# Efficient attention with mixture of depths: q of units 5 to 15 loaded as two shifted copies and transposed by VectorE

## The chip, the cores and the metric

The kernel runs on one core of one Trainium2 chip. The metric is the device time of one execution in microseconds (us). The kernel before took 209.97 us (median of 3 runs, 209.13 to 210.23).

## The reference

Two steps. The first is an attention that takes no scores between queries and keys: q is softmaxed over its 64 features, k over the 576 tokens, k and v are multiplied into a 64 x 64 matrix for each head, and q is multiplied with that matrix. The second is a mixture of depths: a gate scores the 576 tokens of a batch, and only the 128 best go through a two-layer MLP, whose result is added to their rows.

```python
q, k, v: (8 batches, 8 heads, 576 tokens, 64), float32
q_s = softmax(q, axis=features);  k_s = softmax(k, axis=tokens)
kv  = einsum('bhsd,bhse->bhde', k_s, v)
x   = einsum('bhsd,bhde->bhse', q_s, kv)     # then (8, 576, 512): heads side by side
scores = x @ w_gate
top = 128 best tokens of each batch
out = x;  out[top] = x[top] + sigmoid(scores[top]) * (relu(x[top] @ w1) @ w2)   # w1 512x1024, w2 1024x512
```

## The kernel before

**Units.** The attention is cut into 16 units of four heads: unit u is half of the heads of one batch, so two units make a batch. Everything is float32, except for small masks. A head's 576 tokens are 64 partitions of T = 9 consecutive tokens each.

**Loads.** `load` (L115) brings k, v and q of a unit into three rotating sets of buffers, `raw` (L105; unit u uses set u % 3). All are issued from SP's queue in program order. From unit 2 on, k and v are loaded with 64 partitions of the tile (every second one) in each of two DMAs, in rows of 1280 and 1024 bytes (L141); q with all 128 partitions, in two DMAs of 5 and 4 tokens a partition (L135). Units 0 and 1 (`FLAT`) are loaded in another form (L129).

**A unit's work.** `k_exp` and `q_exp` take the exps on ScalarE (L268, L276), `v_copy` moves v beside a column of ones (L281). `kv_mm` (L310) multiplies exp(k) with v on TensorE, `kv_out` (L319 to L323) divides by the sums on VectorE and appends the product with the gate. `q_t` turns exp(q) so that features lie on the partitions: for the units from 3 on, 18 transposes of 64x128 on TensorE into PSUM (L349), and two copies from PSUM into `qT` (part 0 by ScalarE, L356; part 1 by ScalarE or, from unit 5 on, by VectorE, L354). `x_mm` (L375) multiplies with the 64x66 result of `kv_out`: 36 products for each unit, of which each has 64 tokens as its weights. `x_sums` and `x_scale` (L389 to L395) divide by the sums, and `x_store` (L405) writes the unit's rows to the output in HBM: two DMAs, each from 64 neighbouring partitions.

**Selection.** After the second unit of a batch, `score` and `score_row` (L414 to L438) lay the scores out, `ranks` compares every score with all others (five compares of 128x576 on VectorE, L446), `hits` and `find` (L463, L473) give the indices of the 128 best, `fetch` (L487) gathers their rows from the output by an indirect DMA on POOL, which has to wait for the batch's two stores.

**MLP.** `turn` (L524) transposes the gathered rows, `mlp1` (L544) and `mlp2` (L554) are the two layers in eight pieces each, `finish` (L567) adds, and `put` (L559) scatters the rows back.

**Order.** The order on every engine is the program's, written out by hand. From s = 3 on (`LAG`) a loop runs one stage for each unit. Stage s transposes unit s (`q_t`), does `kv_mm` of unit s + 1, `x_mm` of unit s, its sums and scaling, then `queues` (L762): the store of unit s, and the loads of k, v and q of unit s + 3, the first of which waits for the last of `x_mm`. Then come the exps of q of unit s + 1 and of k of unit s + 2, and the copy of v of unit s + 2. Pieces of the MLP of an earlier batch lie in between: odd stages hold layer 1 and the ranks, even stages layer 2 and the next `turn`. The units before that stage are written out one by one (L683 to L741), as is stage 3 (L785 to L829).

The core of the loop's stage, where the change falls:

```python
            if here:
                q_t(s, 0)
                q_t(s, 1, on_vector=s > LAG + 1)
            if follows:
                kv_mm(s + 1)
                kv_out(s + 1)
```

The functions that the diff touches, with the line numbers of the profile:

Of the kernel before, what the change touches and what calls it, by code (L numbers as in the profile page):

```python
# [8 lines left out]
F32 = mybir.dt.float32  # L9
BF16 = mybir.dt.bfloat16  # L10
I32 = mybir.dt.int32
AF = mybir.ActivationFunctionType
# [5 lines left out]
def kernel(  # L18
# [23 lines left out]
    nc = tc.nc  # L42
    B, H, S, D = q.shape
    DM, F = moe_w1.shape
    P = 128
    R = 5
    N2 = R - 1
    T = R + N2
    RP = N2 * P + P // 2
# [3 lines left out]
    SD = S * D  # L53
# [18 lines left out]
    const = ctx.enter_context(tc.tile_pool(name="const", bufs=1))  # L72
    ld = ctx.enter_context(tc.tile_pool(name="ld", bufs=3))
    at = ctx.enter_context(tc.tile_pool(name="at", bufs=2))
    xp = ctx.enter_context(tc.tile_pool(name="xp", bufs=2))
    md = ctx.enter_context(tc.tile_pool(name="md", bufs=2))
# [3 lines left out]
    def bank(tag, bufs):  # L80
        return ps.tile([P, 512], F32, tag=tag, name=tag, bufs=bufs)

    def pair(tag, bufs=1):
        return ps.tile([P, 2, 512], F32, tag=tag, name=tag, bufs=bufs)
# [4 lines left out]
    def part(i):  # L89
        return slice(64 * i, 64 * i + 64)  # L90
# [7 lines left out]
    NU = len(units)  # L98
# [2 lines left out]

    LD = 3
    FLAT = 0, 1
    RR = 4 * R
    raw = {w: [const.tile([P, 2 * T if w == "q" else RR, D], F32, name=f"{w}{n}") for n in range(LD)] for w in "qkv"}  # L105

    def view(t, paired):
        return t.rearrange("p (h r) d -> p h r d", h=4) if paired else t[:, :2 * T].rearrange("p (i r) d -> p i r d", i=2)
# [6 lines left out]
    def load(u, which, after=None, split=False, flat=False):  # L115
        b, qd = units[u]
        for what in which:
            src = {"q": q, "k": k, "v": v}[what]
            first = src[place(b), 4 * qd].offset
            dmas = []  # L120
            if flat:
                t = view(raw[what][u % LD], False)
                if split:
                    for h, queue in enumerate((nc.scalar, nc.sync)):
                        dmas.append(queue.dma_start(out=t[:, h].rearrange("p r d -> p (r d)"),
                                                    in_=bass.AP(tensor=src.tensor, offset=first + 2 * h * SD,
                                                                ap=[[T * D, P], [1, T * D]])))
                else:
                    dmas.append(nc.sync.dma_start(out=t.rearrange("p i r d -> p i (r d)"),  # L129
                                                  in_=bass.AP(tensor=src.tensor, offset=first,  # L130
                                                              ap=[[T * D, P], [2 * SD, 2], [1, T * D]])))
            elif what == "q":
                t = view(raw[what][u % LD], False)
                for r0, r1 in ROWS:
                    dmas.append(nc.sync.dma_start(out=t[:, :, r0:r1].rearrange("p i r d -> p i (r d)"),  # L135
                                                  in_=bass.AP(tensor=src.tensor, offset=first + r0 * D,
                                                              ap=[[T * D, P], [2 * SD, 2], [1, (r1 - r0) * D]])))
            else:
                t = view(raw[what][u % LD], True)
                for n, rows in ((1, N2), (0, R)):  # L140
                    dmas.append(nc.sync.dma_start(out=t[n::2, :, :rows].rearrange("p h r d -> p h (r d)"),  # L141
                                                  in_=bass.AP(tensor=src.tensor, offset=first + n * R * D,
                                                              ap=[[T * D, 64], [SD, 4], [1, rows * D]])))
            if after is not None:
                behind(dmas[0], after)
                after = None
        return dmas[-1]

    ROWS = (0, R), (R, T)
    ctx.enter_context(tc.manual_schedule())  # L150
    load(0, "k", split=True, flat=True)
    load(0, "vq", flat=True)

    def clear(u):
        for what in "kv":
# [5 lines left out]
                                               ap=[[DM, 1], [1, DM]]))  # L161
# [18 lines left out]
    ones_b = const.tile([P, 4 * P], BF16, name="ones_b")  # L180
    nc.vector.memset(ones_b, 1.0)
    w_ps = bank("mm", 2)
    ones_f = const.tile([P, 4 * P], F32, name="ones_f")
    nc.gpsimd.memset(ones_f, 1.0)
    for n in range(WARM):
        nc.tensor.matmul(out=w_ps, lhsT=ones_f[:, :P], rhs=ones_f, start=True, stop=True)
# [20 lines left out]
    for n in range(2):  # L207
        t = const.tile([P, RR, D + 1], F32, name=f"v_ones{n}")
        nc.vector.memset(t[:, :, D:], 1.0)
        v_ones.append(t)  # L210
        t = const.tile([P, 2, C], F32, name=f"kv_w{n}")
        nc.vector.memset(t[:, :, D:D + 1], 1.0)
        kv_w.append(t)
    qrec = const.tile([P, NU, 2, G], F32, name="qrec")
    krec = const.tile([P, NU, 2], F32, name="krec")


    order_minus_p = const.tile([P, RP], F32, name="order_minus_p")
    nc.gpsimd.iota(order_minus_p, pattern=[[1, RP]], base=0, channel_multiplier=-1,
                   allow_small_or_imprecise_dtypes=True)  # L220

# [39 lines left out]
    st = {}  # L261
# [9 lines left out]
    def q_exp(u, c):  # L271
        if c == 0:
            st["qe", u] = at.tile([P, T, 2, D], F32, tag="qe", name="qe")
        r0, r1 = ROWS[c]
        qr = raw["q"][u % LD].rearrange("p (i r) d -> p r i d", i=2)
        nc.scalar.activation(out=st["qe", u][:, r0:r1], in_=qr[:, r0:r1], func=AF.Exp)  # L276

    def v_copy(u, engine=nc.scalar):
# [44 lines left out]
        nc.vector.reduce_sum(out=kw[:, :, D + 1], in_=prod, axis=AX.X)  # L323


    copies = []

    def q_t(u, c, on_vector=False, wide=False, later=False):
# [29 lines left out]
    def x_mm(u, a, wide=False, tag="x"):  # L358

        qT = st["qT", u] if a == 0 else st.pop(("qT", u))  # L360
        x = pair(tag, 2 if tag == "x" else 1)
        kw = kv_w[u % 2]
        for r in range(R):
            for i, c in QUARTERS:
                to = x[part(c), i, r * C:(r + 1) * C]
                if r == N2 and c:
                    last = nc.tensor.matmul(out=to, lhsT=ones_b[part(i), :D], rhs=ones_b[part(i), :C], start=True, stop=True)
                    continue
                if wide and r < N2:
                    if c == 0:  # L370
                        nc.tensor.matmul(out=x[:, i, r * C:(r + 1) * C],
                                         lhsT=qT[part(i), a, r].rearrange("p c t -> p (c t)"), rhs=kw[part(i), a],
                                         start=True, stop=True)
                    continue
                nc.tensor.matmul(out=to, lhsT=qT[part(i), a, r, c], rhs=kw[part(i), a], start=True, stop=True)  # L375
        st["x", u, a] = x[:, :, :R * C].rearrange("p i (r c) -> p i r c", r=R)
        return last

# [113 lines left out]
    def select(b, n, r):  # L492

        k0, m = slots[n]
        if r == 0:
            st["select", n] = bank("mm", 2), md.tile([P, R, P], F32, tag="hit_f", name="hit_f", bufs=1)
        t_ps, hit = st["select", n]
        far = md.tile([P, P], F32, tag="far", name="far")
        nc.scalar.activation(out=far[:, :m], in_=slot_no[:, k0:k0 + m], func=AF.Abs, scale=-1.0,
                             bias=st["rank", b][:, r:r + 1])  # L500
        nc.scalar.activation(out=hit[:, r, :m], in_=far[:, :m], func=AF.Relu, scale=-1.0, bias=1.0)
        row = xs[b][:, r].rearrange("p n i a d -> p (n i a d)")
        for d in range(KD):
            nc.tensor.matmul(out=t_ps[:, d * m:(d + 1) * m], lhsT=row[:, d * P:(d + 1) * P], rhs=hit[:, r, :m],
                             start=(r == 0 and d == 0), stop=(r == N2 and d == KD - 1), skip_group_check=True)
        if r == N2:
            turned(b, n, t_ps)
# [74 lines left out]
    def each(step, b, *args):  # L582
        for n in range(n_sl):
            step(b, n, *args)
# [93 lines left out]
    for h in range(2):  # L678
        nc.tensor.matmul(out=g_ps[part(h), :4 * D], lhsT=ones_f[:1, :D],
                         rhs=w_row.rearrange("o (n i x) -> o i n x", i=2, x=2 * D)[:, h], start=True, stop=True)  # L680
# [61 lines left out]
    LAG = 3  # L742
# [3 lines left out]
    for s in range(LAG, NU + LAG):  # L746
# [5 lines left out]
        def pieces(n, to=None):  # L752
            nonlocal f_next
            for _ in range(n if to is None else max(0, to - f_next)):
                each(piece, mlp_b, f_next)
                f_next += 1

        here, follows = s < NU, s + 1 < NU
        ends = s // 2 if here and s % 2 == 1 else None
# [18 lines left out]
        def rows():  # L778
            score_row(ends)

        def ranks(n0=0, n1=R):
            for r in range(n0, n1):
                compare(ends, r)
# [46 lines left out]
        else:  # L830
            if chosen is not None and s not in AFTER:
                pieces(1 if here else 2)
                search()
            if here:
                q_t(s, 0)
                q_t(s, 1, on_vector=s > LAG + 1)
            if follows:
                kv_mm(s + 1)
                kv_out(s + 1)
# [21 lines left out]
            pieces(0, to=2 if follows else 3)  # L861
            if ends is not None:
                rows()
                ranks()
            if s + 2 < NU:
                k_exp(s + 2)
            pieces(0, to=4)
# [4 lines left out]
                number = count_good(good)  # L872
            if ends is not None:
                each(hits, ends)
            pieces(0, to=KF - 1)
            if second and mlp_b + 1 < B:
                each(turn, mlp_b + 1)
# [35 lines left out]
```

## Time and profile before

| | |
|---|---|
| Median of 3 runs | 209.97 us |
| The profiled execution | 210.15 us, its span 208.4 us |
| Busy: TensorE (PE) | 193.6 us, 93% |
| Busy: VectorE (DVE) | 119.0 us, 57% |
| Busy: ScalarE (ACT) | 92.1 us, 44% |
| Busy: GpSimd (POOL) | 32.4 us, 16% |
| DMA | 46.66 MB, 224 GB/s over the span |
| Time to landing of a q load | 6.2 us (median) |

The profile is that of one execution. The span runs from its first to its last instruction, and the execution's time holds 1.75 us more. Busy times of different engines overlap, so they do not add up to the span. "PE" are the matmuls, "PEld" the loads of their weights. A group of instructions is written as line, engine, operation, what it writes and reads, shape and count; then its busy time in us, the mean in ns of one, and the idle time of the engine ahead of it with what ended most of it. A window gives the busy time of PE, PEld, VectorE, ScalarE and GpSimd, then the share of TensorE's clock, the mean busy share of the 16 DMA engines, and GB/s. In the row of 40 slices one digit is a tenth of busy share.

### The profile page before, as it was taken

Reading aid. Unit: us, or ns where it says so; the run is one execution under the profiler, and the core shown is the slowest. Engines: PE = TensorE matmul, PEld = TensorE weight load, DVE = VectorE, ACT = ScalarE, POOL = GpSimd, SP = SyncE. Lnnn points to the kernel's source line nnn. Section 1 sums busy time; section 2 is a strip of 40 time slices with the busy share of each in tenths; the row PEclk is TensorE's granted clock in tenths of the full one; section 3 lists DMA queues with packets and bytes.
Section 4 is the critical chain, followed back from the end, with each engine's and each line's share of the span. In section 5 each row is a group of like instructions: output and inputs, shape, how many; then the busy total and the mean of one; then the engine's idle time right before and its main releaser. Section 6 shows DMA issues by size and latency. Waiting matters only on the chain.

```text
span 208.4 us, 6943 instructions
## 1 busy us (share of the span) xinstructions
PE 193.6 (93%) x2955; PEld 148.8 (71%) x2955; DVE 119.0 (57%) x361; ACT 92.1 (44%) x135; POOL 32.4 (16%) x93
## 2 busy tenths in 40 slices
PE   7899799798989999999999999999999999999960
PEld 3486789785579848985698759974898579659520
DVE  6668735597167645776378717862776537714010
ACT  3468876574526624545434813672464022111100
POOL 5103000202010101210120104010211012126010
PEclk9999999999999999999999999999999999999995
DMA  6999999999786999995989779895880433131101
GB/s 218 397 307 330 384 360 372 371 381 329 193 296 158 309 327 250 283 279 170 233 282 253 231 175 304 212 314 129 256 247 4 103 110 74 48 101 53 58 5 53
DMA packets 37720, 46.66 MB, mean 224 GB/s; under 512 B 2353, under 2 KB 33073, under 8 KB 37682
## 3 DMA queue, kind: packets, MB, share of 16 engines
q1 hardware_dynamic: 36256, 41.66, 65.2%
q0 software_dynamic: 1280, 4.20, 5.7%
q8 instruction: 25, 0.41, 0.8%
q10 hardware_dynamic: 146, 0.30, 0.5%
q14 instruction: 13, 0.11, 0.2%
HBM read 34.61 MB, written 11.53 MB: 221 GB/s over the span
## 4 chain that ended last, share of the span: by engine, by line
PE 74%; DMA 16%; SPq 3%; issue 1%; ACT 1%; DVE 1%; POOL 0%; POOLq 0%; ACTq 0%
PE mm L544 25%; PE mm L554 25%; DMA k<-in_k_dram 15%; PE x L375 8%; PE kv L310 8%; PE x L349 4%; DMA xr<-out_dram,idx 2%; SPq L141 2%; PE kv L432 2%; PE mm L524 2%; SPq L135 1%; ACT ke L268 1%; PE mm L473 1%; SPq L169 0%; SPq L129 0%
## 5 line engine op out<-in xcount | busy, mean ns | idle before, releaser
L544 PE MATMUL mm<-xT,w 128*128 128x128 f32 x512 | 62.0, 278 | 0.3 <-DVE xT L532 0.3
L544 PEld LDWEIGHTS mm<-xT,w 128*128 128x128 f32 x512 | 58.8, 192 | 2.0 <-ACT xT L532 0.6
L554 PE MATMUL mm<-w,hT 128*128 128x512 f32 x128 | 59.3, 599 | 0.0
L446 DVE SCALAR_TENSOR_TENSOR junk<-srow,s,not_before 128x576 bf16<-128x576 f32 x40 | 32.7, 819 | 9.4 <-ACT srow L438 8.1
L554 PEld LDWEIGHTS mm<-w,hT 128*128 128x128 f32 x128 | 22.6, 190 | 20.6 <-issue 20.1
L567 DVE SCALAR_TENSOR_TENSOR o<-mm,g,xr 128x512 f32<-128x512 f32 x7 | 5.3, 751 | 35.6 <-PE mm L554 35.6
L395 DVE TENSOR_TENSOR xs<-x,qrec 128x640 f32<-128x640 f32 x31 | 24.1, 815 | 0.0
L375 PE MATMUL x<-kv_w,qT 64*64 64x66 f32 x1084 | 21.9, 222 | 1.7 <-issue 1.5
L268 ACT ACTIVATE ke<-k 128x1280 f32<-128x1280 f32 (+1 forms) x16 | 20.0, 1253 | 4.6 <-DMA k<-in_k_dram 4.6
L276 ACT ACTIVATE qe<-q 128x640 f32<-128x640 f32 (+1 forms) x32 | 20.1, 676 | 3.3 <-DMA q<-in_q_dram 3.3
L375 PEld LDWEIGHTS x<-kv_w,qT 64*64 64x64 f32 x1084 | 19.4, 134 | 3.0 <-issue 2.0
L310 PE MATMUL kv<-v_ones,ke 128*64 128x65 f32 x560 | 19.4, 224 | 1.1 <-ACT srow L438 1.1
L310 PEld LDWEIGHTS kv<-v_ones,ke 128*64 128x64 f32 x560 | 17.5, 137 | 2.3 <-ACT srow L438 1.3
L547 ACT ACTIVATE hT<-mm 128x512 f32<-128x512 f32 x16 | 9.6, 597 | 21.5 <-PE mm L544 21.5
L281 ACT COPY v_ones<-v 128x1280 f32<-128x1280 f32 x14 | 17.6, 1257 | 0.7 <-DMA v<-in_v_dram 0.4
L532 ACT COPY xT<-mm 128x512 f32<-128x512 f32 x7 | 4.1, 585 | 30.1 <-PE mm L524 30.1
L487 POOL DMA_INDIRECT xr<-out_dram,idx x8 | 8.3, 1036 | 53.4 <-PE x L349 22.6
L559 POOL DMA_INDIRECT out_dram<-o,idx x7 | 7.0, 996 | 58.9 <-DVE o L567 58.9
L356 ACT COPY qT<-x 128x640 f32<-128x640 f32 (+1 forms) x17 | 11.4, 682 | 9.5 <-PE x L349 8.7
L438 ACT ACTIVATE srow<-kv 128x576 f32<-128x576 f32 x7 | 4.5, 648 | 23.0 <-PE kv L432 23.0
L349 PEld LDWEIGHTS x<-ident,qe 64*128 64x128 f32 x234 | 8.3, 138 | 4.9 <-ACT xT L532 4.5
L354 DVE COPY qT<-x 128x512 f32<-128x512 f32 x11 | 7.6, 692 | 5.8 <-PE x L349 5.8
(115 smaller groups left out, 165.7 us busy)
## 6 DMA issues: line engine op xcount, KB each, us to landing
out_dram<-xs SPq DMA_DIRECT2D x16, 320.0 KB, 3.6
k<-in_k_dram SPq DMA_DIRECT2D x14, 320.0 KB, 5.1
v<-in_v_dram SPq DMA_DIRECT2D x14, 320.0 KB, 6.1
q<-in_q_dram SPq DMA_DIRECT2D x14, 320.0 KB, 6.2
w<-in_moe_w_dram SPq DMA_DIRECT2D x8, 512.0 KB, 7.6
out_dram<-xs SPq DMA_DIRECT2D x16, 256.0 KB, 4.3
k<-in_k_dram SPq DMA_DIRECT2D x14, 256.0 KB, 4.8
v<-in_v_dram SPq DMA_DIRECT2D x14, 256.0 KB, 4.7
```

Of the source, the lines that this page charges most:

```text
L268: nc.scalar.activation(out=ke, in_=view(raw["k"][u % LD], u not in FLAT), func=AF.Exp)
L276: nc.scalar.activation(out=st["qe", u][:, r0:r1], in_=qr[:, r0:r1], func=AF.Exp)
L281: engine.copy(out=out_v, in_=in_v)
L310: nc.tensor.matmul(out=kv_ps[part(i), a, :D + 1], lhsT=ke[:, 2 * i + a, r], rhs=vo[:, 2 * i + a, r], start=(r == 0), stop=(r == N2))
L349: nc.tensor.transpose(out=src[:, a, r], in_=qe[part(a), r0 + r].rearrange("p i d -> p (i d)"), identity=ident[part(a), part(a)])
L356: nc.scalar.copy(out=to, in_=src)
L375: nc.tensor.matmul(out=to, lhsT=qT[part(i), a, r, c], rhs=kw[part(i), a], start=True, stop=True)
L395: nc.vector.tensor_mul(xs[b][:, :, qd, :, a].rearrange("p r i d -> p i r d"), st.pop(("x", u, a))[:, :, :, :D], rec.to_broadcast([P, 2, R, ...
L446: nc.vector.scalar_tensor_tensor(junk, st["srow", b], st["s", b][:, r:r + 1], not_before[:, r], op0=OP.subtract, op1=OP.is_ge, accum_out=s ...
L544: st["piece"] = nc.tensor.matmul(out=h_ps[:, f % 4 * m:(f % 4 + 1) * m], lhsT=w1[:, d, f * P:(f + 1) * P], rhs=xT[:, d, :m], start=(d == 0 ...
L547: nc.scalar.activation(out=hT[:, f - 3:f + 1, :m], in_=h_ps[:, :4 * m].rearrange("p (f c) -> p f c", f=4), func=AF.Relu)
L554: st["piece"] = nc.tensor.matmul(out=st["y", b, n][:m], lhsT=st["hT", b, n][:, f, :m], rhs=w2[:, f], start=(f == 0), stop=(f == KF - 1))
```

## The change

For units 5 to 15 (`TWICE`), q is loaded twice, into a buffer of double size. A head's 576 tokens are now 32 partitions of 18 consecutive tokens; the next 32 partitions hold the same tokens, starting 32 elements (half of a token's 64 features) later. So the first 32 columns of each token hold features 0 to 31 on the first 32 partitions, and features 32 to 63 on the next 32. Four DMAs bring a unit, each with 64 partitions of 1120 elements (4480 bytes). `q_exp` takes the exp of only these first halves, again 2 x 576 elements a partition. The new `q_blocks` transposes them on VectorE in 32x32 blocks, one instruction for each half of the unit, straight into `qT`, which leaves each token's 64 features on 64 partitions. `q_t` is no longer called for these units. `q_blocks(s + 1, ...)` is called in stage s: the first half after the q exps, ahead of the ranks where there are any; the second half straight after it, or after `hits` in stages that have ranks. The half of q's buffers that is now added also serves earlier as the place of `ones_f`, `order_minus_p`, `hit_f` and `far`, which had tiles of their own.

```diff
+    TWICE = range(5, NU)
     RR = 4 * R
-    raw = {w: [const.tile([P, 2 * T if w == "q" else RR, D], F32, name=f"{w}{n}") for n in range(LD)] for w in "qkv"}
+    raw = {w: [const.tile([P, 4 * T if w == "q" else RR, D], F32, name=f"{w}{n}") for n in range(LD)] for w in "qkv"}
+
+    spare = {n: raw["q"][n].rearrange("p r d -> p (r d)")[:, 2 * T * D:] for n in range(LD)}
...
+            elif what == "q" and u in TWICE:
+                t = raw[what][u % LD].rearrange("p (a n) d -> p a (n d)", a=2)
+                for a in range(2):
+                    for i in range(2):
+                        dmas.append(nc.sync.dma_start(out=t[part(i), a, :ROW],
+                                                      in_=bass.AP(tensor=src.tensor, offset=first + (2 * i + a) * SD,
+                                                                  ap=[[D // 2, 2], [2 * T * D, 32], [1, ROW]])))
             elif what == "q":
...
+    ROW = 2 * T * D - D // 2
...
-    ones_f = const.tile([P, 4 * P], F32, name="ones_f")
+    ones_f = spare[2][:, :4 * P]
...
+    for n in range(LD):
+        nc.gpsimd.memset(spare[n][:, ROW:], 0.0)
...
-    order_minus_p = const.tile([P, RP], F32, name="order_minus_p")
+    order_minus_p = spare[2][:, 4 * P:4 * P + RP]
...
     def q_exp(u, c):
         if c == 0:
             st["qe", u] = at.tile([P, T, 2, D], F32, tag="qe", name="qe")
+        if u in TWICE and u not in FLAT:
+            half = raw["q"][u % LD].rearrange("p (a n) (h s) -> p a n h s", a=2, h=2)[:, c, :, 0]
+            to = st["qe", u].rearrange("p r i d -> p (r i d)").rearrange("p (a n s) -> p a n s", a=2, n=2 * T)
+            nc.scalar.activation(out=to[:, c], in_=half, func=AF.Exp)
+            return
...
+    def q_blocks(u, a):
+        if u not in TWICE:
+            return
+        if a == 0:
+            st["qT", u] = at.tile([P, 2, R, 2, D], F32, tag="qT", name="qT")
+        to = st["qT", u].rearrange("p a r c d -> p a (r c d)")[:, :, :T * D].rearrange("p a (j t e) -> p a e j t", j=T, e=2)
+        qe = st["qe", u].rearrange("p r i d -> p (r i d)").rearrange("p (a e j s) -> p a e j s", a=2, e=2, j=T)
+        nc.vector.transpose(out=to[:, a], in_=qe[:, a])
...
     def x_mm(u, a, wide=False, tag="x"):
...
+        by_token = qT.rearrange("p a r c d -> p a (r c) d")
...
-                nc.tensor.matmul(out=to, lhsT=qT[part(i), a, r, c], rhs=kw[part(i), a], start=True, stop=True)
+                rows = by_token[part(i), a, R * c + r] if u in TWICE and u not in FLAT else qT[part(i), a, r, c]
+                nc.tensor.matmul(out=to, lhsT=rows, rhs=kw[part(i), a], start=True, stop=True)
...
-            st["select", n] = bank("mm", 2), md.tile([P, R, P], F32, tag="hit_f", name="hit_f", bufs=1)
+            st["select", n] = bank("mm", 2), spare[1][:, :R * P].rearrange("p (r t) -> p r t", r=R)
...
-        far = md.tile([P, P], F32, tag="far", name="far")
+        far = spare[1][:, (R + r % 2) * P:(R + r % 2 + 1) * P]
...
-            if here:
+            if here and s not in TWICE:
                 q_t(s, 0)
-                q_t(s, 1, on_vector=s > LAG + 1)
+                q_t(s, 1)
...
             if ends is not None:
                 rows()
+            if follows:
+                q_blocks(s + 1, 0)
+            if ends is not None:
                 ranks()
+            else:
+                q_blocks(s + 1, 1)
...
             if ends is not None:
                 each(hits, ends)
+                q_blocks(s + 1, 1)
```

More of the change, by code (lines that the diff above doesn't have):

```diff
@@ L273, in q_exp @@
             st["qe", u] = at.tile([P, T, 2, D], F32, tag="qe", name="qe")
+        if u in TWICE and u not in FLAT:
[3 more added lines that the diff above has]
+            return
         r0, r1 = ROWS[c]
-        qr = raw["q"][u % LD].rearrange("p (i r) d -> p r i d", i=2)
+        qr = raw["q"][u % LD][:, :2 * T].rearrange("p (i r) d -> p r i d", i=2)
         nc.scalar.activation(out=st["qe", u][:, r0:r1], in_=qr[:, r0:r1], func=AF.Exp)
```

## The prediction

> **What bounds the kernel now.** I read the chain of work that ended last first, since it says whose time is the run's time. Then the costliest groups, for the price of what is removed, and the slices and windows, for the DMA engines.
>
> ```profile
> PE 74%; DMA 16%; SPq 3%; issue 1%; ACT 1%; DVE 1%; POOL 0%; POOLq 0%; ACTq 0%
> ...
> L375 PE MATMUL x<-kv_w,qT 64*64 64x66 f32 x1084 | 21.9, 222 | 1.7 <-issue 1.5
> ...
> L349 PEld LDWEIGHTS x<-ident,qe 64*128 64x128 f32 x234 | 8.3, 138 | 4.9 <-ACT xT L532 4.5
> L354 DVE COPY qT<-x 128x512 f32<-128x512 f32 x11 | 7.6, 692 | 5.8 <-PE x L349 5.8
> ```
>
> The loads carry the chain for the first 40 us (DMA 16%, the q, k and v of the first units); after that TensorE is the bound. The transposes to be removed are L349's: 18 for each unit, 13 units. The chain in order of time shows what one unit's transposes are worth on that path:
>
> ```profile
> 113.09 0.86 PE mm L554 x2
> 114.13 0.71 PE x L349 x18
> 114.84 1.32 PE kv L310 x40
> ```
>
> 0.71 us, and 0.18 us idle ahead of them (113.95 to 114.13). So a unit has about 0.89 us of L349 on the path. VectorE and ScalarE are busy 57% and 44% and have room. The DMA engines are the third resource, and the fullest:
>
> ```profile
> DMA  6999999999786999995989779895880433131101
> ```
>
> Nine tenths or more in most slices up to about 150 us. The windows say what that share carries:
>
> ```profile
> 30.00:40.00 10.00, 9.86 (x257) 9.39 (x254) 6.06 (x22) 5.91 (x10) 0.92 (x5) 1.00 1.07 369
> 107.00:117.50 10.50, 10.50 (x197) 9.55 (x195) 7.64 (x21) 6.95 (x10) 1.62 (x4) 1.00 0.90 258
> 117.50:129.50 12.00, 12.00 (x170) 8.12 (x171) 6.75 (x20) 3.88 (x6) 1.93 (x6) 1.00 0.75 220
> 131.20:134.20 3.00, 3.00 (x30) 3.00 (x29) 2.89 (x8) 2.37 (x3) 0.00 (x0) 1.00 0.92 192
> ```
>
> The last two columns are the mean busy share of the 16 engines and GB/s. Two units in steady state (107 to 129.5 us) use 0.90 x 10.5 + 0.75 x 12 = 18.5 us of all 16 engines, so 9.2 us for a unit that TensorE finishes in 11.2. The last line is a stretch that holds only stores of xs, each from 64 neighbouring partitions: engines 92% busy, yet 192 GB/s, against 369 GB/s where loads over all 128 partitions run.
>
> [...] The trace's best slice, 397 GB/s, is 24.8 GB/s for each of 16; I use 24.8.
> [...]
>
> **The change, part by part.**
>
> *TensorE.* 11 units x 18 = 198 of L349's 234 matmuls go: 11 x 0.89 = 9.8 us off TensorE's path. x_mm keeps its count and its 64x64 weights.
>
> *ScalarE and VectorE.* Eleven copies of 692 ns leave each (L356, L354). VectorE gains 22 transposes of 128x576 f32. The nearest row is L395 (128x640 f32, 815 ns), so 815 x 576/640 = 0.73 us each; [...]. VectorE has 14.0 us busy in the 22.2 us of two units (129.5 to 151.7): it loses 2 x 0.69, gains 4 transposes, and becomes the bound only from (22.2 - 12.6)/4 = 2.4 us each. Half a unit's transpose also delays the ranks: q_blocks(s + 1, 0) comes ahead of them, where VectorE idles 1.07 us for srow before the first compare (130.79 us), which covers it. The exps keep their 1152 elements a partition. I put all this at 0; TensorE covers it.
>
> *Start.* Three memsets of 32 columns on POOL, and ones_f, order_minus_p, hit_f and far in the unused half of q's buffers. Their readers are done by about 30 us; the first doubled load into q2 is issued at 39 us, that into q1 at 57 us. 0.
>
> *SP.* Two q issues for a unit become four, 22 more of about 0.5 us; SP idles several us in each unit. 0 as issues, but see next.
>
> *The q loads.* Each of the four DMAs has source dimensions 2, 32, 1120 and a destination of 64 partitions by 1120. The slowest source dimension is 2. [...] each runs on two engines, and on the same two every time. A unit's q is then 4 x 64 x 4480 B = 1.147 MB, 573 KB for each of the two: at 24.8 GB/s 23.1 us [...]. The same two engines also carry their sixteenth of k, v, the stores and the gathers. q is a quarter of the bytes behind the 9.2 us, so the rest is 7 us. **A unit costs those engines about 30 us where TensorE takes 11.** [...]
>
> Nothing covers that. These DMAs, k and v and the stores are behind one another in SP's queue; queues(s) issues x(s), k, v(s + 3), q(s + 3) after x_mm(s), so two units of loads always stand ahead. q_exp(u) waits for its q, and ScalarE is then held in front of k_exp, v_copy and the MLP's evacuations, VectorE in front of ranks; TensorE idles some 20 us for each unit.
>
> Sum. The first such load follows the stores at 38.83 us:
>
> ```profile
> 38.83 1.73 SPq L135 DMA_DIRECT2D q<-in_q_dram  x2
> 40.65 1.63 SPq L405 DMA_DIRECT2D out_dram<-xs  x2
> 42.56 1.89 SPq L141 DMA_DIRECT2D k<-in_k_dram  x2
> ```
>
> Unit 5's q lands at 41 + 23 = 64 us, unit 15's at 64 + 10 x 30 = 364. Behind it in the queue is unit 13's store (2 to 3 us to land), which batch 6's gather needs (1.0 us on POOL, 4.8 to land), so that turn comes 9 us later. Before, the turn of batch 6 starts at 167.2 us and the span ends at 208.4: 41.2, less 0.9 for unit 15's transposes, 40.3. 364 + 9 + 40 = 413 us of span. The profiled execution lasted 210.15 us, 1.75 more than its span, and the median of the runs is 209.97: 415 us.
>
> One term is open on both sides. [...] by the 192 GB/s at 0.92 busy, 13.0 GB/s each, so 44 us for a unit's q instead of 23. If that held for all eleven units, 415 + 11 x 21 = 646. [...] I charge half a unit's contention, 10 us: **425 us**.
>
> **Rivals.**
> - *All sixteen engines serve the load* (the split follows the 64 partitions of the destination). For: no trace of before shows k = 2, and loads and stores with 64 outermost run wide. Against: the source's outer 2. Then q takes 1.147 MB/369 GB/s = 3.1 us of the engines in place of 2.2, so 10.1 a unit, just under TensorE's 11.2 - 0.9 = 10.3. Time 210 - 9.8 = 200, with some waits for late k 202: **faster**. With k engines the unit needs 1147/(24.8k) + 7 us; that stays under 11.2 from k = 11, so sixteen decides for faster and eight (12.8) already for slower.
> - *VectorE becomes the bound*: [...] At 3.0 us each, VectorE needs 12.6 + 12 = 24.6 us for two units instead of 22.2, so 5.5 x 2.4 = 13 us: 223. Nothing in the profile speaks for it; it also needs sixteen engines.
> - [...]
>
> **How the numbers follow.** Two engines: 0.90, most of it between 415 and 500, with a thin part up to 646. Sixteen engines and faster: 0.07. Sixteen with nothing gained, or VectorE or DMA as a mild bound: 0.03, of which 0.01 within 0.5% (about what a measurement of this kernel can tell from no change). [...] The upper end, 630, takes in contention in nearly every unit. Left out: 0.10 of other cases, and about 0.1 of the two-engine one at its edges.
>
> **What would show it.** Right: q's time to landing 20 us or more instead of 6.2; the chain mostly DMA q<-in_q_dram from 60 us on; the mean DMA share falling to a third while the run lengthens; ACT qe waiting for q about 15 us for each unit; qe's starts 28 to 50 us apart; DVE transposes near 0.73 us. Wrong: q landing in 5 to 9 us means that the loads are spread, and the time is then near 202[...].

## The result, and the profile after

The kernel after takes **401.5 us** (median of 4 runs, 400.41 to 401.65); the kernel before took 209.64 us beside it (median of 4). The ratio is 1.914 (95% interval 1.907 to 1.921). The profiled execution after has a span of 399.9 us. The forecast was 425 us, with a range of 366 to 630.

The lines have moved: q's load is now L139, its exp L290, VectorE's transpose L351, `x_mm` L404, the gather L516, the store L434, `turn` L553, the two MLP layers L573 and L583.

First the shares of the chain of waits that ended last, by engine and then by line:

```profile
DMA 70%; PE 16%; SPq 7%; ACT 3%; DVE 2%; issue 1%; POOL 0%; POOLq 0%; ACTq 0%; DVEq 0%
DMA q<-in_q_dram 60%; DMA out_dram<-xs 8%; PE mm L573 5%; SPq L434 4%; PE mm L583 3%; SPq L139 3%; DMA xr<-out_dram,idx 2%; PE mm L533 1%; PE x L404 1%; ACT qe L290 1%; PE mm L197 1%; PE x L369 1%; PE kv L328 1%; ACT srow L467 1%; PE kv L323 1%
```

Before, this line began with PE 74% and DMA 16%. Now q's loads alone are 60% of the run. The same chain in order of time (start, length, what):

```profile
97.12 26.81 DMA q<-in_q_dram
...
124.01 0.69 ACT qe L290
...
184.15 27.85 DMA q<-in_q_dram
...
327.20 24.77 DMA q<-in_q_dram
...
352.05 0.69 ACT qe L290
...
354.23 3.44 DMA xr<-out_dram,idx
...
357.81 1.09 PE mm L553 x4
```

Each load of q stands on the chain for 25 to 28 us, and the exp (`ACT qe`) follows when it lands. The second exp of unit 5 starts at 67.39 us, that of unit 15 at 352.05: 28.5 us for a unit. After that comes the end that the prediction described: unit 15's exp, a gather, the `turn` of batch 6 at 357.81, and the rest of the MLP.

The slices, and two windows of this steady part (the first number after the span's length is PE's busy time; the last three are the granted clock, the mean busy share of the DMA engines, GB/s):

```profile
PEclk9989995597775695865695955875955967759997
DMA  8999444244244356243352352451443432413110
```

```profile
156.20:241.40 85.20, 37.06 (x461) 25.59 (x461) 23.77 (x65) 15.07 (x20) 3.35 (x9) 0.70 0.38 112
241.40:352.00 110.60, 50.51 (x652) 37.57 (x652) 30.92 (x84) 19.30 (x25) 6.70 (x18) 0.72 0.37 110
```

From 40 us on (the fifth digit of the slices) the DMA share falls from 9 to about 4 tenths, and 112 GB/s flow where 369 did, while q's loads are what everything waits for. A third of the engines' time busy and yet a DMA bound: that fits a few busy engines, and the packet records (below) count them. The wait list says who stands still (total us, times, longest):

```profile
ACT qe L290 <- DMA q<-in_q_dram: 198.6, 22, 12.4
POOL xr L516 <- DMA q<-in_q_dram: 194.0, 5, 44.1
PE mm L553 <- DMA xr<-out_dram,idx: 117.9, 7, 20.8
```

ScalarE waits 198.6 us for q in 22 waits. The two waits below it are what follows from that: the stores that a gather needs are issued from the same queue, behind loads of q (the releaser named is q's DMA), and TensorE's `turn` waits 117.9 us for gathered rows. The groups of the exp and of the new transposes:

```profile
L290 ACT ACTIVATE qe<-q 128x576 f32<-128x576 f32 x22 | 15.0, 683 | 198.6 <-DMA q<-in_q_dram 198.6
...
L351 DVE STREAM_TRANSPOSE qT<-qe 128x576 f32<-128x576 f32 x22 | 17.1, 776 | 87.3 <-ACT qe L290 87.3
```

The exps cost what they did (683 ns; 676 before). The transposes cost 776 ns each, 17.1 us in all, and their idle time is that of the exps: VectorE is not what is late.

### The profile page after: what moved, and what is told of

Same layout as the page of the kernel before. It is cut to its first block, busy times and chain, and to the rows that moved or that the text cites. A ratio compares the mean times of both kernels' runs of the same rounds, so it can differ in the third digit from the quotient of the medians.

```text
span 399.9 us, 6589 instructions
## 1 busy us (share of the span) xinstructions
PE 212.3 (53%) x2757; PEld 157.9 (39%) x2757; DVE 128.6 (32%) x372; ACT 87.2 (22%) x124; POOL 32.6 (8%) x96
## 4 chain that ended last, share of the span: by engine, by line
DMA 70%; PE 16%; SPq 7%; ACT 3%; DVE 2%; issue 1%; POOL 0%; POOLq 0%; ACTq 0%; DVEq 0%
DMA q<-in_q_dram 60%; DMA out_dram<-xs 8%; PE mm L573 5%; SPq L434 4%; PE mm L583 3%; SPq L139 3%; DMA xr<-out_dram,idx 2%; PE mm L533 1%; PE x L404 1%; ACT qe L290 1%; PE mm L197 1%; PE x L369 1%; PE kv L328 1%; ACT srow L467 1%; PE kv L323 1%
## 5 line engine op out<-in xcount | busy, mean ns | idle before, releaser
L583 PE MATMUL mm<-w,hT 128*128 128x512 f32 x128 | 69.9, 686 | 57.2 <-ACT hT L576 57.2
L553 PE MATMUL mm<-ident,xr 128*128 128x128 f32 x28 | 7.1, 406 | 117.9 <-DMA xr<-out_dram,idx 117.9
L573 PE MATMUL mm<-xT,w 128*128 128x128 f32 x512 | 62.4, 279 | 0.3 <-DVE xT L561 0.3
L573 PEld LDWEIGHTS mm<-xT,w 128*128 128x128 f32 x512 | 59.4, 193 | 3.0 <-ACT xT L561 1.2
L290 ACT ACTIVATE qe<-q 128x576 f32<-128x576 f32 x22 | 15.0, 683 | 198.6 <-DMA q<-in_q_dram 198.6
L583 PEld LDWEIGHTS mm<-w,hT 128*128 128x128 f32 x128 | 25.1, 213 | 78.8 <-ACT hT L576 58.2
L553 PEld LDWEIGHTS mm<-ident,xr 128*128 128x128 f32 x28 | 4.7, 206 | 123.5 <-issue 123.5
L351 DVE STREAM_TRANSPOSE qT<-qe 128x576 f32<-128x576 f32 x22 | 17.1, 776 | 87.3 <-ACT qe L290 87.3
L328 PEld LDWEIGHTS kv<-v_ones,ke 128*64 128x64 f32 x560 | 25.6, 190 | 8.0 <-issue 7.7
L516 POOL DMA_INDIRECT xr<-out_dram,idx x8 | 8.3, 1035 | 241.7 <-DMA q<-in_q_dram 194.0
L328 PE MATMUL kv<-v_ones,ke 128*64 128x65 f32 x560 | 27.8, 278 | 0.0
L596 DVE SCALAR_TENSOR_TENSOR o<-mm,g,xr 128x512 f32<-128x512 f32 x7 | 5.3, 751 | 59.8 <-PE mm L583 59.8
L404 PE MATMUL x<-kv_w,qT 64*64 64x66 f32 x1084 | 22.5, 228 | 1.2 <-ACT ke L281 1.1
L404 PEld LDWEIGHTS x<-kv_w,qT 64*64 64x64 f32 x1084 | 20.2, 140 | 2.8 <-ACT ke L281 1.2
L337 DVE RECIPROCAL krec<-kv 128x2 f32<-128x2 f32 x16 | 2.7, 169 | 29.5 <-PE kv L328 29.0
```

Of the source, the lines that this page charges most:

```text
L290: nc.scalar.activation(out=to[:, c], in_=half, func=AF.Exp)
L328: nc.tensor.matmul(out=kv_ps[part(i), a, :D + 1], lhsT=ke[:, 2 * i + a, r], rhs=vo[:, 2 * i + a, r], start=(r == 0), stop=(r == N2))
L351: nc.vector.transpose(out=to[:, a], in_=qe[:, a])
L404: nc.tensor.matmul(out=to, lhsT=rows, rhs=kw[part(i), a], start=True, stop=True)
L573: st["piece"] = nc.tensor.matmul(out=h_ps[:, f % 4 * m:(f % 4 + 1) * m], lhsT=w1[:, d, f * P:(f + 1) * P], rhs=xT[:, d, :m], start=(d == 0 ...
L583: st["piece"] = nc.tensor.matmul(out=st["y", b, n][:m], lhsT=st["hT", b, n][:, f, :m], rhs=w2[:, f], start=(f == 0), stop=(f == KF - 1))
```

## The experiments

The experiments ran in four groups, each on another chip and with the kernel before beside it: its median was 212.2 us for e1 to e4, 209.48 for e5 to e8, 210.32 for e9 to e11, 212.69 for e12. Ratios are against these.

### The number of engines: outermost dimension 2, 4 and 8

**e2**: the kernel before, with nothing changed but the shape of q's loads for units 5 to 15.

```diff
-                for r0, r1 in ROWS:
+                for r0, r1 in ROWS if u >= 5 else ():
+                    for i in range(2):
+                        dmas.append(nc.sync.dma_start(out=t[:, i, r0:r1].rearrange("p r d -> p (r d)"),
+                                                      in_=bass.AP(tensor=src.tensor, offset=first + 2 * i * SD + r0 * D,
+                                                                  ap=[[SD - D // 2, 2], [T * D, 64], [1, (r1 - r0) * D]])))
...
```

> The kernel before, with nothing of the change but an outermost source dimension of 2 in the q loads of units 5 to 15: the same bytes (not doubled), four DMAs for a unit, the second 64 partitions read 32 elements off, so that the dimensions cannot be merged (those partitions hold other data of q than the reference's). TensorE still transposes. Theory: 295 KB for each of two engines, 64 x (two rows of 1280 and 1024 bytes) each, about 13 us with the rows' own overhead, plus 7 for the rest: 19 to 20 us a unit, the time 41 + 13 + 10 x 19.5 + 49 + 2 = 300 us. Rivals A and B (doubled bytes, buffers, VectorE): 210, since none of these is in it.

Measured 282.65 us (2 runs, 282.04 and 283.27), ratio 1.334 (1.323 to 1.345). Nothing is doubled here, TensorE still transposes, and no instruction of VectorE is new; the new shape of the loads alone costs 70 us (my sum had 300 us, so 88). The wait list of this kernel:

```profile
ACT qe L281 <- DMA q<-in_q_dram: 72.7, 19, 5.2
```

Before, that wait came to 3.3 us in 2 waits.

**e8**: the changed kernel with an outermost 4 in place of 2, the same bytes and the same 64 partitions.

```diff
-                                                                  ap=[[D // 2, 2], [2 * T * D, 32], [1, ROW]])))
+                                                                  ap=[[16 * 544 - D // 2, 4], [544, 16], [1, ROW]])))
```

> As the changed kernel, with the four q DMAs of a unit from a source of outermost dimension 4 in place of 2, same bytes, same 64 partitions each; partitions get other rows of q than the reference asks for. Theory (as many engines as the outermost dimension): 1.147 MB on four engines, 287 KB each at 24.8 GB/s, is 11.6 us, with 5.4 to 7 us of other traffic 17 to 18.6 us a unit: 53 + 10 x 17.8 + 49 = 280, so 270 to 295 us. Rival (the outermost 2 is a special case[...]): 210 to 240 us, as with 8.

Measured 289.11 us (288.08 and 290.14), ratio 1.379 (1.368 to 1.390). Its slices and its exps of q:

```profile
DMA  7999996665555668655666655665555434132101
...
L290 ACT ACTIVATE qe<-q 128x576 f32<-128x576 f32 x22 | 15.0, 683 | 80.2 <-DMA q<-in_q_dram 80.2
```

The waits for q have shrunk from 198.6 to 80.2 us, and the plateau of the DMA share stands at 5 to 6 tenths where two engines gave 4.

**e3 and e11**: an outermost 8, run twice.

```diff
-                                                                  ap=[[D // 2, 2], [2 * T * D, 32], [1, ROW]])))
+                                                                  ap=[[8 * 544 - D // 2, 8], [544, 8], [1, ROW]])))
```

> The changed kernel, its q loads with an outermost source dimension of 8 instead of 2 (8 x 8 rows of 1120 elements, other rows of q than the reference needs, so the values differ; bytes, count and destination of the DMAs are unchanged). Theory: eight engines, 143 KB for each and unit, 5.8 us, plus 7: 12.8 us a unit against TensorE's 10.3, so about 41 + 6 + 10 x 12.8 + 49 + 2 = 226 us, at most 240. If any further dimension in the source made the load slow, whatever its size: near 400.

> The changed kernel with an outermost source dimension of 8, once more (partitions get other rows of q than the reference asks for); the first time two runs lay 10 us apart. Theory (as many engines as the outermost dimension): 5.8 us of q and 5.4 to 7 of other traffic, 11.2 to 12.8 us a unit against TensorE's 10.5 to 11.1: 222 to 240 us. Rival (from 8 engines on the loads are as good as spread): 205 to 212 us.

e3 gave 230.78 and 240.97 us, too far apart for a ratio, so e11 repeats it: 236.6 us (4 runs: 233.54, 235.88, 237.31 and 242.09), ratio 1.127 (1.116 to 1.138). The page of e11:

```profile
DMA  6999999997957899886976979796966333422101
...
L290 ACT ACTIVATE qe<-q 128x576 f32<-128x576 f32 x22 | 14.5, 678 | 9.5 <-DMA q<-in_q_dram 9.5
```

q's own waits are down to 9.5 us. On the chain the gathers now have 15%, four of them of 7.7 to 8.7 us, and q's loads still 9%.

Put together, by the bytes of q that one engine carries for a unit (1147 KB over 2, 4 or 8; in e2 590 KB over 2):

| | KB an engine | time |
|---|---|---|
| after, outer 2 | 573 | 401.5 us |
| e2, outer 2, single | 295 | 282.65 us |
| e8, outer 4 | 287 | 289.11 us |
| e11, outer 8 | 143 | 236.6 us |

e2 and e8 differ in total bytes, in the number of engines and in who transposes, and agree within 7 us: the time goes with the first column. From e8 to the kernel after, 11 x 286 KB more for each engine cost 112 us, which by this estimate is 28 GB/s for one engine; a packet of 4480 bytes in 173 ns is 25.9.

The trace's packet records count the engines more directly. Of the packets of 4480 bytes, which are q's alone, the kernel after has at most two in flight for 97% of the time from the first to the last of them, e8 at most four for 97%, e11 at most eight for 98%; e5 below, spread, reaches 16. The same queue has packets of 4 bytes, 1816 in the kernel after, which is 16 for each of its 108 other DMAs and 2 for each of q's 44 loads. With an outermost 4 there are 1904, so 4 for each of q's loads, with 8 there are 2080, so 8. So at the three sizes that ran, 2, 4 and 8, as many engines served a load of q as its source's outermost dimension says. No other size under 32 was run.

### The doubled bytes, and the width of a load

**e5**: the same 1.147 MB a unit in rows of 4480 bytes, over 128 partitions.

```diff
-                    for i in range(2):
-                        dmas.append(nc.sync.dma_start(out=t[part(i), a, :ROW],
...
-                                                                  ap=[[D // 2, 2], [2 * T * D, 32], [1, ROW]])))
+                    dmas.append(nc.sync.dma_start(out=t[:, a, :ROW],
+                                                  in_=bass.AP(tensor=src.tensor, offset=first + a * D // 2,
+                                                              ap=[[2 * T * D, P], [1, ROW]])))
```

> As the changed kernel, with the same doubled bytes of q for units 5 to 15 (1.147 MB a unit, rows of 4480 bytes), but loaded by two DMAs over all 128 partitions, outermost source dimension 128; the rows that the partitions get are not those that the reference asks for. Theory [...]: 1.147 MB at 369 GB/s is 3.1 us, so about 10 us of all engines a unit under the 11.1 us that two units of the single load showed for each: the time of the single load plus little, 209 to 214 us. Rival (the bytes themselves cost, and the four DMAs of 32 partitions at 229 us showed mostly that): 225 us or more, with the 4480-byte rows again near 314 ns each.

Measured 206.15 us (5 runs, 205.09 to 206.79), ratio 0.983 (0.978 to 0.988), a little under the 209 to 214 that I expected. **The doubled bytes are not what made the change slow.**

**e1**: the same bytes and rows, in four loads of 32 partitions each, which puts every datum where the changed kernel has it.

```diff
-                for a in range(2):
-                    for i in range(2):
-                        dmas.append(nc.sync.dma_start(out=t[part(i), a, :ROW],
...
+                for i in range(2):
+                    for s in range(2):
+                        p0 = 64 * i + 32 * s
+                        dmas.append(nc.sync.dma_start(out=t[p0:p0 + 32, :, :ROW],
+                                                      in_=bass.AP(tensor=src.tensor, offset=first + 2 * i * SD + s * D // 2,
+                                                                  ap=[[2 * T * D, 32], [SD, 2], [1, ROW]])))
```

> The changed kernel with the same bytes in the same places, but each of the four DMAs of a unit brings both heads of one block of 32 partitions: source dimensions 32, 2, 1120, so nothing is outermost but the 32 partitions. Theory (the outermost 2 confines each load to two engines): [...] the time falls from 401 to near 202 us. [...] as the stores' 192 GB/s suggested, a unit's q takes 5.5 us of all engines and a unit 12.5 us: about 220 us. Rival A (the doubled bytes themselves, or the shifted rows, are what costs): stays near 400. Rival B (the new buffers' or VectorE's waits): stays near 400.

Measured 228.85 us (4 runs, 228.06 to 229.32), ratio 1.079 (1.072 to 1.086): 172 of the change's 192 us are undone by loads with an outermost 32, and some 20 us above e5 are left (0.096 of the time before, by the ratios). That is more than both of my figures, 202 and 220, of which the 220 was an estimate from the stores' 192 GB/s. The slices of e1, and its main queue beside e5's (packets, MB, share of 16 engines over the span):

```profile
DMA  6999999999994999999997899999999141421101
...
q1 hardware_dynamic: 33792, 47.79, 73.6%
```

```profile
q1 hardware_dynamic: 33440, 47.78, 71.4%
```

The same 47.8 MB take 0.736 x 227.2 = 167 us of all engines in e1 and 0.714 x 203.2 = 145 us in e5: 22 us more, about the difference in time. The trace's packet records say which packets: those of 4480 bytes take 314 ns (median) in e1, 173 in e5 and also 173 in the kernel after. So a packet took 1.8 times as long where all engines write 32 neighbouring partitions. The 192 against 369 GB/s of before, for stores from 64 neighbouring partitions and loads over 128, points the same way. What makes the packets longer was not shown: e1 also reads its rows in another order than e5, and the next run warns.

**e9**: e1, with the loads of partitions 64 to 127 issued from ScalarE's queue.

```diff
-                        dmas.append(nc.sync.dma_start(out=t[p0:p0 + 32, :, :ROW],
+                        dmas.append((nc.sync, nc.scalar)[i].dma_start(out=t[p0:p0 + 32, :, :ROW],
```

> The kernel with four loads of 32 partitions each (228.85 us), two of the four (the unit's second pair of heads, partitions 64 to 127) issued from ScalarE's queue in place of SP's, so that an engine has loads to both halves of the partitions at hand at one time. Theory ([...] the rows slowed from 173 to 314 ns): with two queues the rows of the two halves mix[...]: 212 to 222 us. Rival (the engines take up the rows of both queues in step[...]): 226 to 231 us as before, or slower by ScalarE's 22 issues of about 0.5 us.

Measured 232.97 us (4 runs, 232.59 to 233.55), ratio 1.110 (1.102 to 1.118), slower than e1. My theory of mixing fails:

```profile
q1 hardware_dynamic: 32032, 41.48, 62.8%
...
q10 hardware_dynamic: 1906, 6.61, 11.8%
```

74.6% of 231.2 us, 172 us of all engines: nothing was saved (the 4480-byte packets still take 294 ns). The rival, 226 to 231 us or slower by ScalarE's issues, fits; whether the engines kept in step, or some other limit holds them, stays open.

### What the missing transposes are worth

**e4 and e10**: the changed kernel with q loaded once, two DMAs over 128 partitions of 576 elements; the same kernel twice.

```diff
-                    for i in range(2):
-                        dmas.append(nc.sync.dma_start(out=t[part(i), a, :ROW],
...
+                    dmas.append(nc.sync.dma_start(out=t[:, a, :T * D],
+                                                  in_=bass.AP(tensor=src.tensor, offset=first + 2 * a * SD,
+                                                              ap=[[T * D, P], [1, T * D]])))
...
```

The part left out lets `q_exp` read these 576 elements as they lie.

> The changed kernel, but q loaded once, in two DMAs of 128 partitions x 576 elements, and the exp taken of these (so features and tokens are not where the reference has them): same exps, same VectorE transposes, no doubled bytes, no narrow loads. It shows what the transposes' move is worth alone. Theory: TensorE loses 11 x 0.89 = 9.8 us of its path and nothing else takes its place, 200 us. Rival (VectorE's transposes, or the waits of x_mm for them, take the gain back): 205 to 215.

> The single wide load of q once more (features and tokens not where the reference has them). Its profile showed TensorE standing 0.38 us by an issue gap in each unit, a two-unit cycle of 22.28 us as before the change; the doubled load over all partitions, with the same instructions on TensorE in the same order, shows no such gap and 21.07 us. Theory A (the gap belongs to that execution or chip, not to the kernel): cycle 21.1 us and a time of 204 to 207 us where the kernel before takes 209.5. Theory B (the gap comes with the single load): cycle 22.3 us again, 208 to 210 us.

e4 took 209.11 us (4 runs, 208.29 to 210.9), ratio 0.985 (0.979 to 0.992); e10 201.98 us (4 runs, 201.08 to 202.53), ratio 0.963 (0.955 to 0.970). The chain of e10 over two units:

```profile
108.60 0.86 PE mm L582 x2
109.46 0.18 PE mm L501 x5
109.65 1.32 PE kv L327 x40
...
129.47 0.86 PE mm L582 x2
```

And before:

```profile
113.09 0.86 PE mm L554 x2
113.95 0.19 PE mm L473 x5
114.13 0.71 PE x L349 x18
...
135.37 0.86 PE mm L554 x2
```

From 108.60 to 129.47 two units take 20.87 us; before, from 113.09 to 135.37, 22.28. So a unit gains 0.70 us: the 0.71 us of the transposes, and nothing for the 0.18 us ahead of them, which are no gap but five products of `find` (L473, in e10 L501). e10's time came out under both ranges that I had named for it; its cycle is theory A's.

The chain of e4 over the same stretch shows most of why it gained only 3 us:

```profile
114.11 0.86 PE mm L582 x2
...
115.15 1.32 PE kv L327 x40
...
117.12 0.03 PE x L394
117.14 0.17 PE x L403 x4
117.32 0.38 issue
117.70 0.84 PE x L403 x32
...
136.39 0.86 PE mm L582 x2
```

Two units again take 22.28 us. TensorE stands 0.38 us under "issue" in `x_mm`, and the products around it are slower, in every unit from about 72 us on, near the same place of the program. e5, with the same instructions on TensorE in the same order, shows no such gap. The profiled runs of e4 and e10 lie 9.4 us apart (spans of 209.1 and 199.7): 5.8 come after the product pair that e4 reaches at 79.94 us and e10 at 76.34, the other 3.6 before it, and what costs those isn't shown.

**e6**: e4, with the 18 transposes of a unit back at their old place, their results unused.

```diff
+            elif here:
+                for r0, r1 in ROWS:
+                    idle = pair("x", 2)
+                    for r in range(r0, r1):
+                        for a in range(2):
+                            nc.tensor.transpose(out=idle[:, a, (r - r0) * D:(r - r0 + 1) * D], ...
```

> As the single wide load (209.1 us), with the 18 transposes on TensorE of each unit from 5 on put back at their old place, their results unused; qT still comes from VectorE. Theory A (TensorE loses the 0.7 us a unit anyhow, to a stall that the transposes used to fill): no change, 208 to 211 us. Rival B (transposes are a true cost of TensorE, and something of VectorE's path took the gain away): 11 x 0.7 us more, 215 to 219 us.

Measured 209.68 us (20 runs, 208.77 to 212.04), ratio 1.002 (0.999 to 1.005). Its chain:

```profile
113.85 0.86 PE mm L582 x2
114.71 0.18 PE mm L501 x5
114.89 0.70 PE x L870 x18
115.60 1.32 PE kv L327 x40
...
136.13 0.86 PE mm L582 x2
```

22.28 us for two units without an issue gap, with 0.70 us for the transposes. The time lies in theory A's range, and against e4 this looked like a stall that merely fills the transposes' place. But e4's stall came with its group: against e10 (20.87 us) it is rival B, 0.70 us a unit, 7.7 us for 11 units.

**e7**: the kernel before without the transposes; ScalarE and VectorE copy exp(q) unturned.

```diff
+        if u >= 5 and u not in FLAT:
+            (nc.vector.tensor_copy if on_vector else nc.scalar.copy)(
+                out=to, in_=qe[:, r0:r1].rearrange("p r i d -> p i r d"))
+            return
```

> The kernel before, with the transposes of q left out for units 5 to 15: ScalarE and VectorE copy exp(q) as it lies into qT, so x_mm multiplies data that were not turned. No VectorE transposes, loads as before. Theory A (what TensorE gains by the missing transposes comes back as a stall in its own instruction stream, whoever prepares qT): 206 to 211 us. Rival B (VectorE's transposes or their waits ate the gain of the single wide load): 11 x 0.89 us less, 199 to 203 us.

Measured 203.78 us (4 runs, 202.39 to 204.26), ratio 0.970 (0.964 to 0.977); two units take 20.95 us:

```profile
111.17 0.86 PE mm L558 x2
...
132.12 0.86 PE mm L558 x2
```

e10 and e7 agree within their intervals, though on different chips. So what TensorE gains doesn't depend on who prepares `qT`, and VectorE's transposes cost nothing that these intervals can tell.

**e12**: q loaded once and spread, and the shift made by ScalarE: eight exps of 32 partitions in place of two of 128.

```diff
...
-            half = raw["q"][u % LD].rearrange("p (a n) (h s) -> p a n h s", a=2, h=2)[:, c, :, 0]
+            rows = raw["q"][u % LD].rearrange("p (a n) (h s) -> p a n h s", a=2, h=2)[:, 0]
...
-            nc.scalar.activation(out=to[:, c], in_=half, func=AF.Exp)
+            for i in range(2):
+                for e in range(2):
+                    p0, p1 = 32 * (2 * i + c), 64 * i + 32 * e
+                    nc.scalar.activation(out=to[p1:p1 + 32, c], in_=rows[p0:p0 + 32, :, e], func=AF.Exp)
```

> The changed kernel with q of units 5 to 15 loaded once: two DMAs over all 128 partitions, 32 partitions with 18 tokens for each head, nothing doubled. The shift between partitions is made by ScalarE instead: eight exps of 32 partitions x 576 for a unit in place of two of 128 x 576, each from a head's 32 partitions to the 32 where its half of the features belongs. VectorE transposes as in the change. Theory (the gain of the missing TensorE transposes is kept where the load is spread and ScalarE has room): six exps more of 0.67 us, 4.0 us a unit on ScalarE, which is busy 42% of 200 us in the single load; about 8.8 us of a unit's 10.45, so TensorE still bounds: 202 to 207 us, faster than before (210). Rival (ScalarE's longer queue makes the evacuations of the MLP, srow and the exps of k late, each held up to 4 us): 1 to 2 us a unit, 212 to 225 us.

Measured 211.69 us (6 runs, 209.87 to 213.11), ratio 0.9945 (0.9889 to 1.0001): not shown to be faster, where I had expected 202 to 207. ScalarE's slices and the exps, then two units of its chain:

```profile
ACT  3568736784999499849986889669984712111100
...
L293 ACT ACTIVATE qe<-q 32x576 f32<-32x576 f32 x88 | 59.8, 680 | 1.2 <-ACT g L545 0.2
```

```profile
114.37 0.86 PE mm L586 x2
...
117.59 0.41 issue
...
136.72 0.86 PE mm L586 x2
```

The exps cost what I priced, 680 ns, and ScalarE has room (59.8 us for the 88). ScalarE is not on the chain in this stretch; the two units take 22.35 us with the issue gap of e4 in each. So here it was the step "TensorE still bounds at 10.45 us a unit" that failed, and not by ScalarE's queue, as the rival had it. From 50 to 65 us ScalarE's exps do lie on the chain, 4% of the span; yet e12 is at the same product pair at 80.10 us where e4, without the added exps, is at 79.94.

The gap appeared in the groups where the kernel before took 212.2 and 212.7 us (in e1, e3, e4 and e12), and in no profile where it took 209.5 and 210.3. e4 and e10 are one program on either side, so the program alone doesn't decide it. The group alone may not either: e2, in e4's group but with the transposes in place and long waits for q, shows none. What the gap is, no profile here names.

## Why the prediction was right

**Two engines** (0.90 in the forecast): in the prediction an assumption that no trace of before showed. It is shown now, by one kernel that has only the outer 2 (e2, 282.65 us), by two smaller doses of it (e8, 289.11, and e11, 236.6), and by the packets in flight, at most two for 97% of the time. That all four loads of a unit share the same two fits: they stand in the queue together, and their packets are still two at a time.

**23.1 us a unit for q**: right. q's packets took 508 us in all, which is 23.1 us for each of two engines in each of 11 units. **7 us for the rest, 30 together**: measured 28.5 a unit, which leaves 5.4. This term was too high, by 16 us over ten units. That the two engines carry an even sixteenth of the other transfers was an estimate: the packet records name no engine.

**The lower end of the range, 366 us**: it rested on a faster rate of one engine, which was not shown.

**Landings at 64 and 364**: 67.4 and 352.05.

**The turn 9 us after q, and 40.3 us from there**: 5.8 us (352.05 to 357.81) and 42.1. The gather did come behind q, but its own landing took 3.44 us, not 4.8; the sum, 47.9 against 49.3, holds.

**The contention of the two engines, 10 us**: this step failed. The 13.0 GB/s for each engine, 44 us for a unit's q, was an estimate from the stores' 192 GB/s, and half a unit of it a guess. 92% of q's packets take under 180 ns in the kernel after (median 173), so the slowing that was charged didn't come. By the packet records the two engines are not in step from unit 6 on: the second starts on a unit's rows 2.1 to 5.1 us after the first, which at 173 ns is 12 to 29 rows. In unit 5 they start 0.44 us apart, and most of its rows took 173 ns too. Whether two engines in step slow each other, no run shows.

Of the 23.5 us by which 425 was too many, about 10 are this charge, 16 the ten units and 1.4 the end, less 3.4 by which unit 5 landed late.

**TensorE's 0.89 us a unit**: mis-sized. 0.71 are the transposes; the 0.18 before them were `find`'s products (the line at 113.95 above), which I took for idle time. They stay. 11 x 0.70 = 7.7 us, against 9.8. It did not matter for the result, where TensorE waits, but for the rival.

**The rival with sixteen engines, 202 us**: the load without doubling gives 201.98; with the doubled bytes, spread, 206.15. My 0.9 us more of the engines a unit mixed two rates: by the packet records a unit's q takes 3.2 us of all 16 engines in e5 and 1.7 in e10, 1.5 more. In time the doubled bytes cost some 4 us against e10 (the difference of the ratios, 0.0206, is 4.3), and 2.4 against e7, whose loads are single and which ran on e5's chip. Where they are lost isn't shown. e5's chain has two gathers that e10's hasn't:

```profile
50.55 5.70 DMA xr<-out_dram,idx
...
71.03 7.95 DMA xr<-out_dram,idx
```

But e7's has two like them, of 4.91 us at 50.73 and 7.67 us at 70.49, without doubled bytes.

**Eight engines already slower**: right in sign; 12.8 us a unit against 11.2 would be 16 to 18 us over ten or eleven units, and e11 has 26, the gathers' waits among them.

**VectorE**: 0.73 us for a transpose, measured 0.776 (0.758 in e10). It is no bound here: VectorE's share is 32% after and 63% in e10. **The signs that the prediction named**: a mean DMA share of a third (0.37 and 0.38 in the windows), ScalarE waiting 198.6/11 = 18 us a unit where 15 was named, exps 28.5 us apart, at the lower end of 28 to 50. The page after gives no time to landing for q's loads; the chain's 25 to 28 us stand in for it.

**ScalarE, start, SP's issues at 0**: nothing in e5, e7 or e10 asks for more. In the kernel after SP's issues are 7% of the chain (last section).

## What to carry to other kernels

Read the outermost dimension of a DMA's source before its bytes: in this case a 2 in a source of the same bytes was worth some 170 to 195 us (against e1 and e5), and it shows in a profile as a low mean DMA share together with a chain made of one load. Then look how many partitions the engines write at one time: doubled bytes over 128 cost some 2 to 4 us, over 32 some 20 us more (in e1, which also reads its rows in another order). Where a few per cent are at stake, read every line of the chain between two that you subtract, and run a kernel on more than one chip before giving a gap a cause.

## What the runs showed of the hardware that was not expected

- The clock granted to TensorE was lower in the runs in which it waited more: 0.764 on average after (the digits 5 to 9 above), 0.858 in e8, 0.882 in e2, 0.931 in e11, 0.995 in e10. No run tests which comes from which. L583's products took 686 ns after, and 599 before.
- SP's issues can take long themselves: from 125.36 to 147.14 us the chain after holds a piece on an issue of q's load (5.35 us) and three on issues of the store (9.09, 2.51 and 4.01 us), where one of q elsewhere (at 124.70) takes 0.62. It happened while two engines had everything queued on them; the profile doesn't say what the issue waits for.
- An exp of 32 x 576 took 680 ns (e12), one of 128 x 576 673 (e10): fewer partitions saved ScalarE nothing.
- The transpose of 128 x 576 float32 on VectorE took 758 to 776 ns, a little more than the 734 ns that its 128 x 640 product of 815 ns gives by size.
